# One value piece split by DMA engines, and the bias in five transfers: attention decode with a dense layer on one core

## The chip, the cores and the metric

The kernel runs on one core of a Trainium2 chip. The metric is device time in microseconds (us) of one execution. Before the change three runs took 191.95, 192.65 and 192.1 us; the median is 192.1 us.

## What is computed

One token for each of two sequences goes through a layer norm. Its result feeds an attention over the last 4096 positions of a key and value cache, and a dense layer with the mish activation. Both results are added to the input.

```python
def reference(A_x, A_k_cache, A_v_cache, A_wq, A_wo, B_x, B_w1, B_b1, B_w2):
    def _A_ref(x, k_cache, v_cache, wq, wo):
        ...
        W = min(4096, max(256, Sk // 4))
        q = (x @ wq).reshape(B, Sq, Hq, Dh).transpose(0, 2, 1, 3)
        k = jnp.repeat(k_cache[:, :, Sk - W:, :], rep, axis=1)
        v = jnp.repeat(v_cache[:, :, Sk - W:, :], rep, axis=1)
        p = _softmax(jnp.einsum("bhqd,bhkd->bhqk", q, k) * (Dh ** -0.5), axis=-1)
        o = jnp.einsum("bhqk,bhkd->bhqd", p, v)
        return o.transpose(0, 2, 1, 3).reshape(B, Sq, Hq * Dh) @ wo
    def _B_ref(x, w1, b1, w2):
        h = jnp.einsum("bsd,df->bsf", x, w1) + b1
        ...
        return jnp.einsum("bsf,fd->bsd", h * jnp.tanh(sp), w2)
    xn = _layernorm(A_x, axis=-1)
    return A_x + _A_ref(xn, ...) + _B_ref(xn, ...)
```

The sizes: two sequences, width 448, 16 query heads on 8 key heads of 256 values, 4096 positions, and 1792 hidden values in the dense layer; all in bf16.

## The kernel before

The work on the cache is cut into four units (`U`, two key heads of both sequences each, so `J` = 4 rows of the cache). In a unit the keys come in four pieces (`load_k`, L91) and the values in four (`load_v`, L97), each a tile of 128 partitions by 16 KB, 2 MB in all. A value piece `g` holds 1024 positions: partition `4x + j` has 32 tokens in a row (`T`) of the block `x` (32 blocks, `C`) of cache row `j`. All pieces go through rings of buffers: three for keys, four for values, two for wo. `wq` and `w1` borrow buffers of the value ring and `w2` one of the key ring.

The order is written out by hand (`manual_schedule`, L65), and nearly all transfers stand in one queue, that of SP, in the order of the code: two key pieces, wq in two parts, a key piece, w1, a key piece; then for every unit (the loop at L569) the four value pieces, the keys of the next unit, and its part of wo (`load_wo`, L106). In the last unit wo goes first, in two transfers, value piece 3 comes in two parts (L577, L578), and w2 in four parts ends the stream (L580, `load_w2` at L537). Only x and the bias b1 are issued from ACT (L122, L124). The framework gives every transfer one of eight semaphores in turn, so a transfer is issued when the eighth before it has landed. Where it writes a used buffer, it also waits for the buffer's reader.

The compute engines follow the stream. DVE turns every key piece (`turn`, L264, the transposes of L267); PE makes the scores (`scores`, L342), ACT their exponential (L351), DVE turns them (L357). PE then weighs the values: `values` (L381, matmul L389) piece by piece, in matmuls of two tokens each, and `gather` (L400) folds the result. In the last unit, piece 3 takes another way (`values_fixed`, L419, matmul L424), `finish` (L433) divides by the softmax's sum, `mix` (L479) multiplies by wo and `dense_out` (L548) adds the dense layer's second half part by part; both record their matmuls at L247. DVE and ACT copy the result out (L620, L622) and SP stores it (L623).

At the start ACT loads x and the bias and computes the root for the layer norm (L158); DVE goes on from there with small steps to `xs` (L161 to L218), which PE needs for the projection (L289) and for the dense layer's first half (L501). The bias is used at L515, by DVE, after the four key pieces of unit 0 have been turned.

Of the kernel before, what the change touches and what calls it, by code (L numbers as in the profile page):

```python
# [17 lines left out]
def kernel(  # L18
# [13 lines left out]
    nc = tc.nc  # L32
    P = 128
    G = 4
    J = 4
# [3 lines left out]
    _, Hkv, Sk, Dh = A_k_cache.shape  # L39
# [8 lines left out]
    C = P // J  # L48
    CT = W // C
    T = CT // R  # L50
# [35 lines left out]
    def ring(name):  # L86
        return v_pool.tile([P, KE], BF16, tag="v", name=name)
# [3 lines left out]
    def load_k(u, r):  # L91
        t = k_pool.tile([P, KE], BF16, tag="k", name="k")
        src = kview[u][:, s0:, :].rearrange("j (c t) d -> c j (t d)", c=C)
        nc.sync.dma_start(out=t[:], in_=src[:, :, r * KE : (r + 1) * KE])  # L94
        k_t[u, r] = t

    def load_v(u, g, lo=0, hi=T):  # L97
        if lo == 0:
            v_t[u, g] = ring("v")
        t = v_t[u, g]  # L100
        src = vview[u][:, s0:, :].rearrange("j (g x t) d -> g x j (t d)", g=G, x=C)
        nc.sync.dma_start(
            out=t[:, lo * Dh : hi * Dh], in_=src[g, :, :, lo * Dh : hi * Dh]
        )

    def load_wo(u):  # L106
        w = wo_pool.tile([P, KU, rep, 2 * D], BF16, tag="wo", name="wo")
        if u < U - 1:
            nc.sync.dma_start(
                out=w[:].rearrange("p k h e -> p (k h e)"),  # L110
                in_=A_wo.rearrange("(k u y i) d -> u y k (i d)", k=KU, u=U, i=8)[u],
            )
        for k2 in range(KU if u == U - 1 else 0):
            r0 = (u + U * k2) * rep * Dh
            nc.sync.dma_start(  # L115
                out=w[:, k2, :, :],
                in_=A_wo[r0 : r0 + rep * Dh, :].rearrange("(h p c) d -> p h (c d)", h=rep, p=P),
            )
        wo_t[u] = w
# [1 line left out]
    x_bf = consts.tile([Bsz, D], BF16)  # L121
    nc.scalar.dma_start(out=x_bf[:, :], in_=A_x.flatten_outer_dims())  # L122
    b1_sb = consts.tile([P, 2, NI], BF16)
    nc.scalar.dma_start(out=b1_sb[:], in_=B_b1.rearrange("(k q c) -> q k c", k=2, q=P))  # L124

    load_k(0, 0)
    load_k(0, 1)
# [2 lines left out]
    for lo, hi in ((0, 4), (4, NS)):  # L130
        t = ring("wq")
# [14 lines left out]
    for k in range(KU):  # L146
        nc.gpsimd.tensor_copy(
            out=hot[:, k, :, :, k], in_=ident[:].rearrange("p (q y) -> p y q", y=4)
# [10 lines left out]
        out=rstd[:], in_=mv[:, 1:2], func=ACT.Sqrt, bias=eps_t[:], scale=1.0  # L159
# [4 lines left out]
        out=xn_bf[:],  # L164
# [8 lines left out]
        out=parm[:], in_=ident[:].rearrange("p (a o) -> p o a", o=2), axis=AXIS.X, op=ALU.add  # L173
# [3 lines left out]
        out=jm[:],  # L177
        in_=ident[:].rearrange("p (a j h) -> p j a h", j=J, h=rep),
# [4 lines left out]
        out=jm[:], in0=jm[:], scalar1=-1.0, scalar2=29952.0, op0=ALU.add, op1=ALU.mult  # L183
# [3 lines left out]
        out=mneg[:], in_=jm[:].unsqueeze(1).to_broadcast([P, TH * 8, J])  # L187
    )
    sel = consts.tile([P, 2, NQ], FP32)
    for x in range(2):  # L190
        for w in range(4):
            at = 32 * w + (2 * (w % 2) + x) * NQ
            src = ident[:, at : at + NQ]
            if w == 0:
                nc.vector.tensor_copy(out=sel[:, x, :], in_=src)
            else:
                nc.vector.tensor_tensor(
                    out=sel[:, x, :], in0=sel[:, x, :], in1=src, op=ALU.add
# [16 lines left out]
    for odd in range(2):  # L215
        for half in range(2):
            o = (half + odd) % 2
            nc.vector.tensor_scalar(  # L218
                out=xs[:, odd::2, half * Bsz : (half + 1) * Bsz],
# [12 lines left out]
    def carry():  # L232
        e_sb = small.tile([P, 2 * Dh], FP32, tag="vs", name="e_sb", bufs=1)[0:Bsz, 0:D]
        nc.scalar.copy(out=e_sb, in_=early[:])
        for g in range(G):
            nc.tensor.matmul(
                acc[32 * g : 32 * g + Bsz, :],
                lhsT=id2[:],
                rhs=e_sb[:, g * DG : (g + 1) * DG],
                start=True,  # L240
                stop=False,
                skip_group_check=True,
            )
# [31 lines left out]
    for n in range(2):  # L275
        for e in range(2):
# [3 lines left out]
                out=sp[:],  # L280
                in_=ident[:, o : o + 63 : 2].unsqueeze(1).to_broadcast([P, G, 32]),
# [47 lines left out]
    def scores(u, i):  # L329
        sc = ps_sc.tile([P, TH, 32], FP32, tag="sc", name="sc")  # L330
        nc.tensor.matmul(  # L331
            sc[:].rearrange("p t m -> p (t m)"),
            lhsT=ident[:],
            rhs=mneg[:].rearrange("p a j -> p (a j)"),
            start=True,
            stop=False,
            skip_group_check=True,
        )
        for n in range(NB):
            for e in range(2):  # L340
                for w in range(4):
                    nc.tensor.matmul(  # L342
                        sc[32 * w : 32 * (w + 1), :, :],
                        lhsT=qd[:, u, 2 * n + e, :, :].rearrange("p g q -> p (g q)"),
                        rhs=ktm[i][:, n, e, :, 32 * w : 32 * (w + 1)],
                        start=False,
                        stop=(n == NB - 1 and e == 1),
                        skip_group_check=True,
                    )
        ex = small.tile([P, TH, 32], BF16, tag="ex", name="ex")  # L350
        nc.scalar.activation(  # L351
            out=ex[:].rearrange("p t m -> p (t m)"),
            in_=sc[:].rearrange("p t m -> p (t m)"),
            func=ACT.Exp,
            scale=scale,
        )
        nc.vector.transpose(  # L357
            out=p_t[i][:].rearrange("p g t q -> p t g q"),
            in_=ex[:].rearrange("p t (g q) -> p t g q", g=G),
        )  # L360
# [84 lines left out]
    def relay(u):  # L445
        oT = state.pop(("oT", u))
        ox_ps = ps_m.tile([P, 4, 2, Bsz], FP32, tag="m", name="ox_ps")
        for h in range(rep):
            rows = slice(h * 64, (h + 1) * 64)
            for y in range(4):  # L450
                for k in range(KU):
                    nc.tensor.matmul(  # L452
                        ox_ps[rows, y, :, :],
                        lhsT=hot[:, k, y, :, :].rearrange("p q k -> p (q k)"),
                        rhs=oT[:, :, k * rep + h, :],
                        start=(y == 0 and k == 0),
                        stop=(y == 3 and k == KU - 1),
                        skip_group_check=True,
                    )
        ox = small.tile([P, 8, Bsz], BF16, tag="ox", name="ox")  # L460
        nc.scalar.copy(
            out=ox[:].rearrange("p i b -> p (i b)"),
            in_=ox_ps[:].rearrange("p y c b -> p (y c b)"),
        )
        state["ox", u] = ox

    def mix_early(u):
        ox = state.pop(("ox", u))
        w = wo_t.pop(u)[:].rearrange("p k h (c d) -> p (k h c) d", c=2)
        for i in range(8):  # L470
            nc.tensor.matmul(  # L471
                early[:],
                lhsT=ox[:, i, :],
                rhs=w[:, i, :],
                start=False,
                stop=(u == U - 2 and i == 7),
            )
# [59 lines left out]
    def load_w2(part):  # L537
        if part == 0:
            state["w2"] = k_pool.tile([P, KE], BF16, tag="k", name="w2")
        k, lo, hi = w2_parts[part]  # L540
        w2_in = B_w2.flatten().rearrange("(k p e) -> k p e", k=2, p=P)
        at = k * NI * D
        nc.sync.dma_start(
            out=state["w2"][:, at + lo * D : at + hi * D],
            in_=w2_in[k, :, lo * D : hi * D],
        )
# [9 lines left out]
    def turns(u, r):  # L556
        for i in range(NH):
            turn(u, r, i)
# [10 lines left out]
    for u in range(U):  # L569
        last = u == U - 1  # L570
        if last:
            load_wo(u)
        load_v(u, 0)
        load_v(u, 1)
        load_v(u, 2)
        if last:
            load_v(u, 3, 0, 24)  # L577
            load_v(u, 3, 24, T)  # L578
            for part in range(len(w2_parts)):
                load_w2(part)  # L580
        else:
            load_v(u, 3)
            load_k(u + 1, 0)
            load_k(u + 1, 1)
            load_k(u + 1, 2)
            load_wo(u)
            load_k(u + 1, 3)
        if u > 0:
            relay(u - 1)
            mix_early(u - 1)  # L590
        if last:
            carry()
        scores(u, 0)
        scores(u, 1)
        weigh(u)
        for g in range(G - 1):
            values(u, g)
        if not last:
            values(u, G - 1)
            turns(u + 1, 0)  # L600
            turns(u + 1, 1)
            gather(u)
            finish(u)
            turns(u + 1, 2)
            turns(u + 1, 3)
    u = U - 1
# [9 lines left out]
    for g in range(G):  # L616
        dst = res[:, g * DG : (g + 1) * DG]
        src = acc[32 * g : 32 * g + Bsz, :]
# [35 lines left out]
```

The softmax here doesn't subtract the row's maximum and nothing guards it: scores larger than these inputs give would overflow.

## Time and profile before

| What | Value |
|---|---|
| Median of three runs | 192.1 us |
| The profiled execution's own time | 192.14 us |
| Its span (first to last instruction) | 190.1 us |
| PE busy | 79.8 us (42%) |
| DVE busy | 91.5 us (48%) |
| ACT busy | 12.3 us (6%) |
| DMA | 77.79 MB, mean 409 GB/s |
| Issue of a value piece on SP (L102), last unit | 541 ns median, five issues from 150.6 to 156.2 us |
| Issue of a part of w2 on SP (L543) | 337 ns median, four issues from 161.2 to 168.4 us |
| Issue of the bias on ACT (L124) | 404 ns; 12.7 us to landing |

Times in the views are microseconds from the span's start. A view by windows gives the busy time of every engine in a stretch, then the clock that was granted to TensorE, the mean busy share of the 16 DMA engines and what they moved. DMA packets are listed by queue: q1 has the transfers that SP issues, q10 those of ACT, q8 and q14 carry instructions. The trace has times and sizes of the packets, but not the number of the engine that moved one. For a transfer it has the times at which its engines report: sixteen events on its semaphore, here called landings.

### The profile page before, as it was taken

How to read it: one execution, taken by the hardware profiler on the slowest of the kernel's cores; microseconds unless marked ns; L12 is line 12 of the kernel's file. 1: busy time of each engine (PE TensorE's matmuls, PEld its weight loads, DVE VectorE, ACT ScalarE, POOL GpSimd, SP SyncE). 2: the span in 40 equal slices, each digit the busy share in tenths (PEclk: the TensorE clock that was granted, in tenths of full speed). 3: DMA queues.
4: the chain of work that ended last, by engine and by line, in shares of the span. 5: the costliest groups of instructions: out<-in, count | busy, mean ns of one | idle time of the engine just before them, and what ended most of it. 6: DMA issues, size and time to landing. Idle time of an engine off the chain costs nothing.

```text
span 190.1 us, 2021 instructions
## 1 busy us (share of the span) xinstructions
PE 79.8 (42%) x873; PEld 37.8 (20%) x873; DVE 91.5 (48%) x97; ACT 12.3 (6%) x23; POOL 4.0 (2%) x16
## 2 busy tenths in 40 slices
PE   0301525197316016296233017394252026575384
PEld 0100115032104012032014012131022021221182
DVE  6887067583001999553003996823006994831001
ACT  3000030011001000011001000020010001020001
POOL 8000000000000000000000000000000000000000
PEclk9999999999965555869955555889755557696555
DMA  6999999999999999999999999999999999999990
GB/s 221 390 435 427 442 418 434 424 422 428 428 431 428 421 427 425 431 434 424 424 428 428 434 421 428 428 431 421 438 424 421 422 433 400 434 428 418 416 377 29
DMA packets 7025, 77.79 MB, mean 409 GB/s; under 512 B 997, under 2 KB 1769, under 8 KB 2537
## 3 DMA queue, kind: packets, MB, share of 16 engines
q1 hardware_dynamic: 6740, 77.66, 96.8%
q8 instruction: 6, 0.10, 0.2%
q10 hardware_dynamic: 276, 0.01, 0.1%
q14 instruction: 3, 0.02, 0.0%
HBM read 77.67 MB, written 0.00 MB: 409 GB/s over the span
## 4 chain that ended last, share of the span: by engine, by line
DMA 85%; DVE 10%; issue 3%; SPq 1%; PE 0%; DVEq 0%
DMA k<-in_A_k_cache_dram 66%; DMA w<-in_B_w_dram 12%; DVE kt L267 10%; DMA wo<-in_A_wo_dram 7%; PE acc L247 0%; SPq L115 0%; SPq L94 0%; DVEq L649 0%; DVE res L620 0%; DVE oT L436 0%
## 5 line engine op out<-in xcount | busy, mean ns | idle before, releaser
L267 DVE STREAM_TRANSPOSE kt<-k 128x2048 f32<-128x2048 f32 x32 | 72.1, 2290 | 55.5 <-DMA k<-in_A_k_cache_dram 55.4
L389 PE MATMUL pv<-v,p 128*32 128x512 bf16 x240 | 19.4, 462 | 25.7 <-DMA v<-in_A_v_cache_dram 25.7
L342 PE MATMUL sc<-kt,qd 128*32 128x512 bf16 x256 | 22.0, 500 | 13.9 <-DVE kt L267 13.9
L389 PEld LDWEIGHTS <-p 128*32 128x32 bf16 x240 | 7.0, 107 | 41.3 <-issue 37.8
L452 PE MATMUL ox_ps<-oT,hot 128*64 128x4 bf16 x48 | 2.3, 192 | 29.7 <-DVE oT L436 29.7
L342 PEld LDWEIGHTS <-qd 128*32 128x32 bf16 x256 | 8.5, 115 | 25.5 <-issue 23.1
L357 DVE STREAM_TRANSPOSE p<-ex 128x512 bf16<-128x512 bf16 x8 | 5.7, 712 | 13.1 <-ACT ex L351 13.1
L471 PE MATMUL early<-wo,ox 128*2 128x448 bf16 x24 | 9.4, 571 | 5.1 <-DMA wo<-in_A_wo_dram 5.1
L409 PE MATMUL o<-sel,vs 128*128 128x8 f32 x32 | 7.5, 363 | 2.9 <-ACT vs L403 2.9
L409 PEld LDWEIGHTS o<-sel,vs 128*128 128x128 f32 x32 | 7.1, 325 | 6.5 <-ACT vs L403 6.5
L289 PE MATMUL q_ps<-wq,xs 128*32 128x512 bf16 x28 | 3.4, 624 | 12.0 <-DMA wq<-in_A_wq_dram 12.0
L452 PEld LDWEIGHTS <-hot 128*64 128x64 bf16 x48 | 2.5, 151 | 29.6 <-issue 29.5
L351 ACT ACTIVATE ex<-sc 128x512 bf16<-128x512 f32 x8 | 4.8, 597 | 39.6 <-PE sc L342 39.6
L436 DVE TENSOR_TENSOR oT<-o,rec 128x16 bf16<-128x16 f32 x4 | 0.6, 145 | 12.7 <-PE o L424 12.7
L403 ACT COPY vs<-pv 128x512 f32<-128x512 f32 x4 | 2.3, 586 | 49.8 <-PE pv L389 49.8
L367 PE MATMUL dn<-p,ones 128*128 128x512 bf16 x8 | 3.1, 383 | 4.5 <-DVE p L357 4.5
L501 PE MATMUL h_ps<-xs,w 128*128 128x4 bf16 x49 | 2.8, 193 | 4.9 <-DMA w<-in_B_w_dram 4.9
L471 PEld LDWEIGHTS <-ox 128*2 128x2 bf16 x24 | 2.8, 115 | 9.6 <-issue 8.5
L331 PE MATMUL sc<-mneg,ident 128*128 128x512 bf16 x8 | 4.1, 514 | 0.0
L210 PE MATMUL xr_ps<-ident,xrows 2*128 2x2 bf16 x7 | 1.0, 180 | 6.6 <-DVE xrows L209 6.6
L289 PEld LDWEIGHTS <-xs 128*32 128x32 bf16 x28 | 1.0, 126 | 13.9 <-issue 13.9
L306 DVE COPY qT<-qt_ps 128x16 bf16<-128x16 bf16 x4 | 0.4, 167 | 6.9 <-PE qt_ps L301 6.9
(62 smaller groups left out, 39.9 us busy)
## 6 DMA issues: line engine op xcount, KB each, us to landing
k<-in_A_k_cache_dram SPq DMA_DIRECT2D x16, 2048.0 KB, 18.0
v<-in_A_v_cache_dram SPq DMA_DIRECT2D x15, 2048.0 KB, 25.1
wo<-in_A_wo_dram SPq DMA_DIRECT2D x3, 896.0 KB, 31.4
wq<-in_A_wq_dram SPq DMA_DIRECT2D x1, 2048.0 KB, 16.2
w<-in_B_w_dram SPq DMA_DIRECT2D x1, 1568.0 KB
wq<-in_A_wq_dram SPq DMA_DIRECT2D x1, 1536.0 KB, 19.3
v<-in_A_v_cache_dram SPq DMA_DIRECT2D x1, 1536.0 KB, 27.8
wo<-in_A_wo_dram SPq DMA_DIRECT2D x2, 448.0 KB, 13.2
```

The lines of the kernel that those rows point to most:

```text
L267: nc.vector.transpose(out=kt[i][:, :, :, r, :], in_=t[:, i * w : (i + 1) * w].bitcast(FP32).rearrange("p (a c j) -> p a c j", c=P // (R * ...
L289: nc.tensor.matmul(q_ps[32 * u : 32 * (u + 1), :], lhsT=xs[:, s, :], rhs=wq_t[s][:, u * 512 : (u + 1) * 512], start=(s == 0), stop=(s == N ...
L331: nc.tensor.matmul(sc[:].rearrange("p t m -> p (t m)"), lhsT=ident[:], rhs=mneg[:].rearrange("p a j -> p (a j)"), start=True, stop=False, ...
L342: nc.tensor.matmul(sc[32 * w : 32 * (w + 1), :, :], lhsT=qd[:, u, 2 * n + e, :, :].rearrange("p g q -> p (g q)"), rhs=ktm[i][:, n, e, :, 3 ...
L351: nc.scalar.activation(out=ex[:].rearrange("p t m -> p (t m)"), in_=sc[:].rearrange("p t m -> p (t m)"), func=ACT.Exp, scale=scale,)
L357: nc.vector.transpose(out=p_t[i][:].rearrange("p g t q -> p t g q"), in_=ex[:].rearrange("p t (g q) -> p t g q", g=G),)
L367: nc.tensor.matmul(dn[:].rearrange("p a q -> p (a q)"), lhsT=ones[:], rhs=p_t[i][:].rearrange("p g t q -> p (g t q)"), start=(i == 0), sto ...
L389: nc.tensor.matmul(pv[32 * w : 32 * (w + 1), :, :].rearrange("p x d -> p (x d)"), lhsT=p_t[a // 4][:, g, 4 * (a % 4) : 4 * (a % 4) + 4, :] ...
L409: nc.tensor.matmul(po[:, c, :], lhsT=sb[:, x, c::2], rhs=sel[:, x, :], start=(x == 0 and c == 0), stop=(last and x == 1), skip_group_check ...
L452: nc.tensor.matmul(ox_ps[rows, y, :, :], lhsT=hot[:, k, y, :, :].rearrange("p q k -> p (q k)"), rhs=oT[:, :, k * rep + h, :], start=(y == ...
L471: nc.tensor.matmul(early[:], lhsT=ox[:, i, :], rhs=w[:, i, :], start=False, stop=(u == U - 2 and i == 7),)
L501: nc.tensor.matmul(h_ps[:, i, :, :].rearrange("p k b -> p (k b)"), lhsT=w1_v[:, s, i, :], rhs=xs[:, s, 0 : 2 * Bsz], start=(s == 0), stop= ...
```

## The change

Value piece 0 of the last unit was one transfer of 32 tokens on 128 partitions. Now its first 26 tokens are one such transfer, and the other six come in four transfers of 32 partitions each (8 blocks by 4 cache rows, 3 KB on a partition). [...] The bias, one transfer of 128 partitions before, comes in five: one of 64 partitions and four of 16. Nothing else is changed; the bytes moved are the same.

```diff
-    def load_v(u, g, lo=0, hi=T):
-        if lo == 0:
+    def load_v(u, g, lo=0, hi=T, x0=0, x1=C):
+        if lo == 0 and x0 == 0:
             v_t[u, g] = ring("v")
         t = v_t[u, g]
         src = vview[u][:, s0:, :].rearrange("j (g x t) d -> g x j (t d)", g=G, x=C)
         nc.sync.dma_start(
-            out=t[:, lo * Dh : hi * Dh], in_=src[g, :, :, lo * Dh : hi * Dh]
+            out=t[J * x0 : J * x1, lo * Dh : hi * Dh], in_=src[g, x0:x1, :, lo * Dh : hi * Dh]
         )
...
-    nc.scalar.dma_start(out=b1_sb[:], in_=B_b1.rearrange("(k q c) -> q k c", k=2, q=P))
+    b1_in = B_b1.rearrange("(k q c) -> q k c", k=2, q=P)
+    for lo, hi in ((0, 64), (64, 80), (80, 96), (96, 112), (112, P)):
+        nc.scalar.dma_start(out=b1_sb[lo:hi], in_=b1_in[lo:hi])
...
-        load_v(u, 0)
+        if last:
+            load_v(u, 0, 0, 26)
+            for x0 in range(0, C, 8):
+                load_v(u, 0, 26, T, x0, x0 + 8)
+        else:
+            load_v(u, 0)
         load_v(u, 1)
         load_v(u, 2)
```

## The prediction

> **What bounds the kernel now.** I read the page's slices and queues first, then the chain that ended last, then the windows of the last microseconds, the instructions there, and last the queue of SP.
>
> The slices, the queues and the chain of the page:
>
> ```profile
> DMA  6999999999999999999999999999999999999990
> q1 hardware_dynamic: 6740, 77.66, 96.8%
> q8 instruction: 6, 0.10, 0.2%
> q10 hardware_dynamic: 276, 0.01, 0.1%
> DMA 85%; DVE 10%; issue 3%; SPq 1%; PE 0%; DVEq 0%
> ```
>
> The DMA engines are busy from the second slice to the last but one, and the chain is 85% DMA. The kernel is one stream of 77.66 MB on q1, and all else hides behind it. So a part of the change counts only if it alters the moment at which the stream ends, or adds work behind that moment. Two rows matter beside q1: q8 moves six packets of instructions, 0.10 MB or 16 KB each, and q10 is the small queue of x and the bias.
>
> How the stream ends, in windows (PE, PEld, DVE, ACT, POOL busy, clock, DMA share, GB/s):
>
> ```profile
> 184.00:184.50 0.50, 0.43 (x17) 0.34 (x13) 0.03 (x1) 0.00 (x0) 0.00 (x0) 0.50 1.14 425
> 184.50:185.00 0.50, 0.30 (x16) 0.30 (x20) 0.14 (x1) 0.00 (x0) 0.00 (x0) 0.50 0.70 264
> 185.00:185.30 0.30, 0.30 (x24) 0.30 (x16) 0.00 (x0) 0.00 (x0) 0.00 (x0) 0.50 0.39 155
> 185.30:185.60 0.30, 0.30 (x28) 0.30 (x20) 0.00 (x0) 0.00 (x0) 0.00 (x0) 0.50 0.34 131
> 185.60:186.00 0.40, 0.40 (x32) 0.40 (x21) 0.00 (x0) 0.00 (x0) 0.00 (x0) 0.50 0.35 130
> 186.60:187.00 0.40, 0.35 (x8) 0.01 (x3) 0.00 (x0) 0.00 (x0) 0.00 (x0) 0.50 0.00 0
> ```
>
> The share falls from full to about 0.35 by 185.3 and stays there until 186: six of sixteen engines still have data. The semaphore events of the trace say the same of each transfer. The last one's sixteen landings are ten from 185.00 to 185.34, then 186.22, 186.48, 186.64, 186.66, 186.86 and 186.95. The lag is old: landings show two late engines at 41 us, three at 66, four at 97, five at 133, six from 168 on. Each step follows a packet on an instruction queue (q14 at 39.7 with 8 KB; q8 at 36.0, 60.3, 91.6, 128.2, 163.6 with 16 KB, about 1.1 us each). A sixth q8 packet, at 184.5, delays none of the landings.
>
> What runs behind the stream (start, time, what):
>
> ```profile
> 178.22 1.90 PE L389 MATMUL pv<-v,p 128*32 128x512 bf16 x16 [2.99 <-DMA v<-in_A_v_cache_dram]
> ...
> 182.58 1.85 PE L424 MATMUL o<-p,v 128*128 128x8 bf16 x64
> 184.47 0.17 DVE L436 TENSOR_TENSOR oT<-o,rec 128x16 bf16<-128x16 f32 x1 [12.74 <-PE o L424]
> ...
> 184.70 0.91 PE L247 MATMUL acc<-wo,oT 128*2 128x112 bf16 x32 [0.27 <-DVE oT L436]
> ```
>
> PE waits for value piece 2 (landed at 178.18) and then works almost without a gap to 187.45. Its last 56 matmuls need about 1.6 us at the 28 ns of the 32 before them, from 185.6 on, so without the last DMA waits it would end near 187.2. Two things thus end together: the stream and PE's work from piece 2 on. Both follow the slow engines, since piece 2 has the same gap (ten landings by 176.56, six up to 178.18).
>
> [...] x, with two rows, has two data packets and two landings. [...] the bias packets lie one between every two 16 KB packets from 4.3 to 13 us. [...]
>
> **The change, part by part.** The sum is made against the profiled execution: 192.14 us, span 190.1, 2.0 around it; the median of the runs shown is 192.1, the same within 0.1.
>
> Value piece 0 of the last unit. Prices are packet start to packet start on one engine: 607 ns for 16384 bytes, 456 for 12288, so 494 for 13312 (26 tokens, between the two); 3072 bytes lie between 1792 (70) and 3584 (136), so 117; the closing 4-byte packet 6.
> - Before, every engine: 8 x 607 = 4.86 us.
> - After, engines 8 to 15: 8 x 494 = 3.95, which is 0.91 less.
> - After, engines 0 to 7: 3.95 + 4 transfers x 4 packets x 117 + 4 x 6 = 5.85, which is 0.99 more.
> Nothing comes between this piece and the end that evens the engines out, so the shift passes whole to piece 2 and to the last transfer.
>
> SP issues four more transfers of 0.54 us (the row of value issues). Every transfer also waits for the eighth before it, by its semaphore. So piece 1 waits for the last key piece (161.1), piece 2 and the first part of 3 for the two wo transfers (162.3, 163.5), the second part and the four w2 transfers for piece 0 and its four small ones (near 168). Before, w2 went out from 161.2 to 168.4; now to about 170. Engines take up piece 1 near 166 and w2 near 183, so over 4 and about 13 us cover it; past that, it would be paid one for one. The output's wait is long over.
>
> Bias. ACT issues four more of 0.40 us: table load and rstd (L158, ending at 3.4) come 1.6 us later, and DVE behind them: its row of small steps ends near 10.0 instead of 8.36, and the first transposes (8.43 to 17.92) shift by as much. Behind these wait PE's projection (idle until wq lands at 18.3) and the issue of key piece 3 (at 12.96, needed at 30.6). DVE waits for the third key piece at 26.87 anyway. Cost nil, cover about 8 us. The bias itself has 16 data packets per engine as before and 4 more closing ones, landing near 17 instead of 14, needed at 40. By the ring of eight, wq part 2 waits for key piece 0 (8.4), key piece 2, w1 and key piece 3 for bias pieces (10 to 15 us): all with over 4 MB queued ahead, and none needed before 18. 8 new transfers in all leave the end's order on the semaphores as it was, but for the small pieces. PE's program and so its q8 packets stay.
>
> So the whole effect is one question: on which side are the six late engines? No row of the profile numbers an engine. Had chance put them, all six among 8 to 15 would be very rare (28 in 8008)[...]. And one of the six was hit by q14[...]. The bounds of the unknown:
> - all six in 8 to 15: late ones end at 186.95 - 0.91 = 186.04, the others at 185.34 + 0.99 = 186.33. 0.62 earlier.
> - the least late one (186.22) in 0 to 7: 187.21, 0.26 later. The middle ones (186.48 to 186.66): 187.5 to 187.65, up to 0.70 later.
> - the latest in 0 to 7: 187.94, 0.99 later.
> [...]
>
> I take both sides, with a middle engine or the least late one in 0 to 7: 0.26 to 0.70, middle 0.5. 192.14 + 0.5 = 192.6.
>
> **The rivals.**
> - Gain: all late engines are the relieved ones. For it: six fit into eight[...]. Against: two queues, and six of eight places. 192.14 - 0.62 = 191.5.
> - Slower, clearly: the latest engine is among 0 to 7, which already end the stream and now carry 0.99 more. It decides from the point where an engine of 0 to 7 lands after 186.9 before the change; price 0.99[...]: 193.1 to 193.8. For it: nothing says that instructions prefer the upper half. Against: only one or two of the sixteen are that late.
> - It doesn't do what it says: the pieces spread over all sixteen engines. Then each has the old bytes and eight more closing or short packets, under 0.1: 192.2. Against it: x's two packets.
>
> **How the numbers follow.** Forecast 0.44 (192.4 to 192.9); gain 0.30 (191.3 to 191.8); slower 0.20 (193.1 to 193.8); nothing 0.06. A measurement of this kernel tells about 0.5%, 0.96 us, from no change: below 191.1 or above 193.1. The gain reaches that only with luck in the runs (they spread over 0.7): 0.04. Slower: 0.20 of the rival and 0.02 of the forecast's tail. Same: 0.74. The range holds gain and forecast and the lower half of the slower case: 191.4 to 193.4. The forecast's own range is 192.4 to 192.9.
>
> **What would show it.** In the last windows, the DMA share would again end in a long step if late engines were loaded, or fall within 0.4 us if they were relieved. The landings of piece 2 and of the last transfer tell the groups: 0.99 later for eight, 0.91 earlier for eight. SP's w2 issues should end near 170, rstd near 5, with key landings up to 158 as before. I am wrong if PE's matmuls at L389 wait less at piece 2 though the stream ends no earlier, if early landings move by over 0.3, or if the small transfers take much more than 117 ns a packet.

## The result, and the profile after

The changed kernel takes 194.64 us (median of six runs, 193.68 to 194.83) where the kernel before takes 192.26 (191.95 to 192.65): a ratio of 1.011, with a 95% interval from 1.009 to 1.014. It is 2.4 us slower. The profiled execution took 194.63 us with a span of 192.9, which is 2.8 more than before. What lies around the span is 1.7 instead of 2.0.

The page of the changed kernel, slices, queues and chain:

```profile
DMA  5999999999999999999999999999999999999960
q1 hardware_dynamic: 6900, 77.66, 96.0%
q8 instruction: 6, 0.10, 0.2%
q10 hardware_dynamic: 340, 0.01, 0.1%
DMA 76%; DVE 11%; PE 5%; issue 3%; ACTq 2%; ACT 1%; SPq 0%; DVEq 0%
```

The bytes of q1 are the same; there are 160 packets more, and 64 closing packets more on q10. Each of the four small transfers has eight landings, so it ran on eight engines. The prediction and the expectations call these engines 0 to 7 and the others 8 to 15; no trace numbers them, and the numbers are names here. That it is the same eight each time is seen with the extra transfers below: four of them to partitions 0 to 63 make eight landings of the next piece 1.7 us later and the other eight 0.2. The chain has gained PE (5%) and lost DMA. The stream is still the bound up to its end, but more stands behind that end.

The same stretch in windows (PE, PEld, DVE, ACT, POOL busy, clock, DMA share, GB/s):

```profile
185.50:186.00 0.50, 0.50 (x25) 0.50 (x22) 0.00 (x0) 0.00 (x0) 0.00 (x0) 0.50 0.78 305
186.00:186.50 0.50, 0.23 (x15) 0.15 (x15) 0.17 (x1) 0.00 (x0) 0.00 (x0) 0.50 0.84 312
186.50:187.00 0.50, 0.50 (x28) 0.50 (x32) 0.00 (x0) 0.00 (x0) 0.00 (x0) 0.50 0.40 133
187.00:187.40 0.40, 0.40 (x28) 0.40 (x20) 0.00 (x0) 0.00 (x0) 0.00 (x0) 0.50 0.09 34
187.40:187.70 0.30, 0.30 (x24) 0.30 (x16) 0.00 (x0) 0.00 (x0) 0.00 (x0) 0.50 0.06 24
187.70:188.20 0.50, 0.50 (x32) 0.41 (x21) 0.00 (x0) 0.00 (x0) 0.00 (x0) 0.50 0.06 23
188.20:188.70 0.50, 0.26 (x12) 0.08 (x1) 0.00 (x0) 0.00 (x0) 0.00 (x0) 0.50 0.01 2
188.70:189.20 0.50, 0.00 (x0) 0.00 (x0) 0.00 (x0) 0.00 (x0) 0.00 (x0) 0.50 0.00 0
```

Before, the share stood near 0.35 (six engines) until 186 and then ran out by 186.6. Now nearly all engines are busy until 186.5, and from 187.4 to past 188 the share is 0.06: one engine of sixteen. The landings of the last transfer say it too: three at 185.29 to 185.64, eleven from 186.85 to 187.32, one at 187.64, one at 188.68.

In the last window PE does nothing either, though all data is there. The instructions of that time, and the last lines of the chain:

```profile
187.14 1.32 PE L249 MATMUL acc<-w,act_bf 128*2 128x112 bf16 x44
189.23 0.45 PE L249 MATMUL acc<-w,act_bf 128*2 128x112 bf16 x12 [0.77 <-DMA w<-in_B_w_dram]
189.23 0.18 PEld L249 LDWEIGHTS <-act_bf 128*2 128x2 bf16 x11 [0.95 <-issue]
189.70 0.56 DVE L627 CAST res<-acc 2x112 bf16<-2x112 f32 x2 [3.32 <-PE acc L249]
189.74 0.51 ACT L629 CAST res<-acc 2x112 bf16<-2x112 f32 x2 [7.19 <-PE acc L249]
190.75 0.29 SPq L630 DMA_DIRECT2D out_dram<-res  x1
```
```profile
186.44 2.02 PE acc L249 x47
188.46 0.77 issue
189.23 0.49 PE acc L249 x12
```

The timeline puts the matmuls' gap down to the DMA of w2. But eight of these twelve matmuls work on w2's third part, which landed at 188.44, and four on its last, which landed at 188.68, 0.55 us before they start. The weight load in front of them waited for nothing that the profile shows ("issue"), and so says the chain. The copies end at 190.27, and SP issues the output only at 190.75. So two stalls follow the stream. From these times, for both profiled executions:

| Step | Before | After | Difference |
|---|---|---|---|
| last landing of w2 | 186.95 | 188.68 | +1.73 |
| then to the start of the last matmuls | 0.04 | 0.55 | +0.51 |
| then to the end of the copies | 1.00 | 1.04 | +0.04 |
| then to the issue of the output | 0.06 | 0.48 | +0.42 |
| then to the output's landing | 1.17 | 1.26 | +0.09 |
| then to the end of the span | 0.87 | 0.84 | -0.03 |

The sum is +2.76, the whole difference of the spans. The experiments take the rows with 1.73, 0.51 and 0.42 one after the other.

### The profile page after: what moved, and what is told of

The parts are those of the page before. It is cut to its first block, busy times and chain, and to the rows that moved or that the text cites. A ratio compares the mean times of both kernels' runs of the same rounds, so it can differ in the third digit from the quotient of the medians.

```text
span 192.9 us, 2031 instructions
## 1 busy us (share of the span) xinstructions
PE 81.5 (42%) x872; PEld 37.9 (20%) x873; DVE 91.3 (47%) x97; ACT 12.3 (6%) x23; POOL 3.9 (2%) x16
## 4 chain that ended last, share of the span: by engine, by line
DMA 76%; DVE 11%; PE 5%; issue 3%; ACTq 2%; ACT 1%; SPq 0%; DVEq 0%
DMA k<-in_A_k_cache_dram 60%; DVE kt L269 9%; DMA v<-in_A_v_cache_dram 9%; DMA wo<-in_A_wo_dram 7%; ACTq L126 1%; PE acc L249 1%; PE pv L391 1%; PE o L411 1%; PE o L426 1%; ACT L160 1%; DVE sel L199 1%; PE xr_ps L212 1%; DVE xs L220 0%; ACT vs L405 0%; ACTq L122 0%
## 5 line engine op out<-in xcount | busy, mean ns | idle before, releaser
L391 PE MATMUL pv<-v,p 128*32 128x512 bf16 x240 | 20.4, 479 | 25.4 <-DMA v<-in_A_v_cache_dram 25.4
L344 PE MATMUL sc<-kt,qd 128*32 128x512 bf16 x256 | 22.7, 511 | 13.9 <-DVE kt L269 13.9
L503 PEld LDWEIGHTS <-w 128*128 128x128 bf16 x49 | 2.7, 154 | 5.0 <-DMA w<-in_B_w_dram 5.0
L377 DVE TENSOR_REDUCE rec<-dn 128x8 f32<-128x512 f32 x4 | 2.8, 692 | 1.9 <-PE dn L369 1.9
```

The source lines that it names most:

```text
L344: nc.tensor.matmul(sc[32 * w : 32 * (w + 1), :, :], lhsT=qd[:, u, 2 * n + e, :, :].rearrange("p g q -> p (g q)"), rhs=ktm[i][:, n, e, :, 3 ...
L391: nc.tensor.matmul(pv[32 * w : 32 * (w + 1), :, :].rearrange("p x d -> p (x d)"), lhsT=p_t[a // 4][:, g, 4 * (a % 4) : 4 * (a % 4) + 4, :] ...
L503: nc.tensor.matmul(h_ps[:, i, :, :].rearrange("p k b -> p (k b)"), lhsT=w1_v[:, s, i, :], rhs=xs[:, s, 0 : 2 * Bsz], start=(s == 0), stop= ...
```

## The experiments

Each kernel is compared with the kernel before as it ran beside it (192.25 to 192.34 us). Times are medians, and a ratio is the time over that of the kernel before.

Four theories are tested first. P: the uneven shares of the engines, made worse since the pieces for partitions 64 to 127 and the transfers of the other eight engines slow each other; this was an assumption, which no run had shown yet. Q: the later start of ACT and DVE, or the shifted order of the semaphores. R: small packets or more transfers are dearer than priced. S: the source blocks 16 to 31 are slow to read. E, I and F came later and are told where they are tested.

### The parts alone

Bias in five, the value piece whole:

> The kernel before with only the bias in five transfers. Theory P (engines 0 to 7 carry more, one of them was already late[...]): nothing at the end, 192.3 us, within 0.3. Theory Q (the loss comes from the longer start of ACT and DVE, or from the shifted ring of semaphores): at least 193.

The pieces alone, the bias whole:

> The changed kernel with the bias in one transfer again. Theory P: the whole loss, 194.5 us, and the first transposes at 8.4 us as before. Theory Q: about 192.6.

The same bytes in as many transfers, but over all engines:

```diff
-            for x0 in range(0, C, 8):
-                load_v(u, 0, 26, T, x0, x0 + 8)
+            for lo, hi in ((26, 28), (28, 30), (30, 31), (31, T)):
+                load_v(u, 0, lo, hi)
```

> The changed kernel, but the six tokens come in four transfers of 128 partitions on all sixteen engines (2, 2, 1 and 1 tokens). Theory P: no loss, 192.3 us. Theory R (small packets, or four more transfers as such, are dearer than priced): over 193.5.

| Kernel | Time, us | Ratio, 95% interval | Last landing of w2 | Span |
|---|---|---|---|---|
| bias in five alone | 192.86 | 1.0017 to 1.0039 | 186.63 | 190.7 |
| pieces alone | 194.94 | 1.0121 to 1.0161 | 189.29 | 193.1 |
| over all engines | 192.94 | 1.0023 to 1.0046 | 186.99 | 191.1 |

The pieces alone carry the whole loss, as P expected. The stream is late only where they go to eight engines: placement, not number or size of transfers. But the first and the last lose 0.6 to 0.7 us with a stream that ends when it did (186.95 before). P expected nothing there and Q at least 0.7 for the bias; the loss stands behind the last landing, which neither theory had in it. R falls with the third run: as many transfers, with packets of 512 and 1024 bytes where the change has 3072, and no later end of the stream.

### Which engines, and what slows them

The changed kernel with the pieces in another order, partitions 64 to 127 first (`for x0 in (16, 24, 0, 8)`):

> The changed kernel with the four pieces in another order: those for partitions 64 to 127 first, those for 0 to 63 last. Theory P: the same time as the changed kernel, 194.6 within 0.4, but the long steps between the landings (1.0 and 0.85 us, the last two pieces before) now belong to the first two pieces, and the last two step by 0.5. Theory R: the steps keep their order, the last two long.

It takes 194.85 us (ratio 1.0097 to 1.0156), as P expected. In the changed kernel the on-time engines land the four pieces near 166.1, 166.7, 167.7 and 168.5: steps of 0.6, 1.0 and 0.8 us. In this one they land near 166.8, 167.6, 168.1 and 168.7: the piece at place two, here one for partitions 64 to 127, takes 0.9, and the two for 0 to 63 take 0.5 and 0.6. The long steps moved with the pieces.

To part destination from source, four extra transfers of the same form (32 partitions x 3 KB, 8 engines) go into an unread buffer behind a whole value piece in the kernel before, once to partitions 0 to 63 from the blocks that the changed kernel loads to 64 to 127, once the other way round:

```diff
         load_v(u, 0)
+        if last:
+            load_spare(u, ((0, 16), (32, 24), (0, 16), (32, 24)))
```

The pairs are first partition and first source block; each transfer takes tokens 26 to 31 of its eight blocks. The other kernel has ((64, 0), (96, 8), (64, 0), (96, 8)).

> The kernel before plus four extra transfers that nobody reads, behind value piece 0 of the last unit, of the changed kernel's shape (32 partitions, 3 KB each, engines 0 to 7), into a spare buffer: all to partitions 0 to 63, read from the source blocks 16 to 31. Theory P[...]: steps of 0.5 us between their landings, eight landings of piece 1 about 1.9 us later, the other eight unmoved; the latest of engines 0 to 7 ends the stream, about 193.5 us. Theory S (the source blocks 16 to 31 make a piece slow): steps of 0.85 to 1.0.

> The same with the places turned round: all four extra transfers go to partitions 64 to 127 and read the source blocks 0 to 15. Theory P: steps of 0.85 to 1.0 us, all sixteen landings of piece 1 later, about 195.5 us, clearly over the one with low partitions. Theory S: steps of 0.5 and the same time as the one with low partitions.

| Extra transfers to | Time, us | Ratio, 95% interval | One transfer | Their eight engines, next piece | The other eight, next piece |
|---|---|---|---|---|---|
| partitions 0 to 63 | 193.72 | 1.0056 to 1.0086 | 0.46 to 0.49 | +1.7 | +0.2 |
| partitions 64 to 127 | 196.72 | 1.0215 to 1.0265 | 0.87 to 0.96 | +3.9 | +2.1 |

The last two columns are the on-time landings of value piece 1 against those of before (171.30 to 171.66). The windows of the two kernels in the time of these transfers, low first:

```profile
166.50:168.00 1.50, 1.50 (x17) 0.33 (x13) 0.02 (x1) 0.60 (x1) 0.00 (x0) 0.67 1.06 434
168.00:170.00 2.00, 1.96 (x33) 0.77 (x22) 0.69 (x1) 0.30 (x1) 0.00 (x0) 1.00 0.98 416
```
```profile
166.50:168.00 1.50, 1.50 (x13) 0.24 (x9) 0.11 (x1) 0.60 (x1) 0.00 (x0) 0.50 1.00 210
168.00:170.00 2.00, 2.00 (x28) 0.80 (x24) 0.60 (x1) 0.00 (x0) 0.00 (x0) 0.62 1.10 247
```

In both the sixteen engines are busy all the time (share 1.0), but with the high destination they move about half: 210 and 247 GB/s instead of 434 and 416. A busy share tells that packets are under way, not how fast. A transfer to the high partitions takes 0.87 to 0.96 us, one to the low 0.46 to 0.49. The other eight engines, which have no part in it, lose 2.1 us with the high destination, about 0.5 for each of the four, and 0.2 in all with the low one.

No trace says which partitions an engine writes, and none shows why the destination counts. What is measured is that transfers to partitions 64 to 127 take twice the time beside whole pieces, and that both groups of engines lose by it (3.9 and 2.1 us, against 1.7 and 0.2). P is confirmed in this; of its two times, 193.5 and 195.5, the first was met and the second passed by 1.2 us. S falls: blocks 16 to 31 are quick when they go to low partitions, and blocks 0 to 15 slow when they go to high ones.

The changed kernel shows the same in the time of its own pieces. The first line is of the kernel before, the others of the changed one:

```profile
168.00:170.00 2.00, 1.25 (x21) 0.42 (x10) 0.47 (x2) 0.60 (x1) 0.00 (x0) 1.00 1.02 434
166.00:167.00 1.00, 1.00 (x13) 0.16 (x5) 0.00 (x0) 0.00 (x0) 0.00 (x0) 0.50 1.05 263
167.00:168.00 1.00, 1.00 (x15) 0.34 (x17) 0.32 (x1) 0.60 (x1) 0.00 (x0) 0.77 1.26 301
168.00:169.00 1.00, 1.00 (x24) 0.44 (x20) 0.40 (x1) 0.00 (x0) 0.00 (x0) 1.00 0.71 261
```

### What is lost behind the last landing

Of SP's instructions in the trace, one comes some 0.45 us late although what it waits for is there: the 80th of those recorded. In the kernel before, the 80th is the wait for the output, the last of five waits at the end, and the output is under way until 189.22 anyway. The five instructions that the pieces add (four issues and a wait) bring the output's own issue onto this place (theory I). To test it, ACT issues the output:

```diff
-    nc.sync.dma_start(out=out.flatten_outer_dims(), in_=res[:])
+    nc.scalar.dma_start(out=out.flatten_outer_dims(), in_=res[:])
```

In the changed kernel, and as a control in the kernel before:

> The changed kernel with its output issued by ACT instead of SP. In the changed kernel SP issues the output 0.49 us after its data is ready, in the kernel before 0.06 us. Theory I (a place in SP's own instruction stream stalls it for about 0.45 us; five more instructions ahead of it have brought the output's issue onto that place): the output goes out within about 0.1 us of the last copy, time about 194.2 (-0.4). If the issue is late because of the data or of the queue of semaphores, it stays at 194.6 with the gap of 0.5.

> The kernel before with its output issued by ACT instead of SP, the control of the changed kernel's run with the same edit. Theory I expects no gain, since SP there has its stall behind the output's issue, while the output is under way: about 192.3 (within 0.2). A gain of 0.4 here as well would mean that ACT's issue is simply quicker than SP's.

The changed kernel takes 194.19 us (ratio 1.0074 to 1.0111), 0.45 less than with SP. That interval overlaps the one with SP (1.0088 to 1.0137), so the medians alone don't show the gain. The trace shows that the wait is gone: the output goes out 0.08 us after the copies, which end at 190.33:

```profile
189.80 0.51 ACT L629 CAST res<-acc 2x112 bf16<-2x112 f32 x2 [7.17 <-PE acc L249]
190.41 0.28 ACTq L630 DMA_DIRECT2D out_dram<-res  x1
```

The control was expected at 192.3 and takes 192.92 (1.0017 to 1.0045). With the output's issue gone SP has fewer instructions ahead of the 80th, which now comes behind the output's landing (189.39): the gap is from 189.49 to 189.92 there, and the span ends 1.33 us after the landing instead of 0.87. The expectation was wrong, since I had forgotten that the edit moves the place; the place itself was confirmed. (The other 0.2 is the matmuls' stall told below: 0.29 here, 0.04 in the kernel before.) Where it falls in each trace:

| Kernel | Gap ahead of SP's instruction | What it holds up |
|---|---|---|
| before | 80 of 85 | the wait for the output: hidden |
| after; over all engines | 80 of 90 | the output's issue: 0.45 |
| after, output by ACT | 80 of 88 | a wait for w2: hidden |
| before, output by ACT | 80 of 83 | the end: 0.43 |
| bias in five alone | 80 of 85 | the end: 0.43 |
| the four extra transfers, either way | 80 of 91 | a wait for a value piece: hidden |

The bias in five leaves SP's program as it was, and yet it shows the gap. There the reason is the order of the end (theory E, a form of Q). SP waits at the end for the transfer semaphores in a fixed order, with five instructions. Four more transfers move the output to another semaphore, which is waited for first; the other four waits, 0.07 us each, and the gap come behind its landing (189.17) instead of ahead of it: the span ends 1.55 us after the landing. To test this, four transfers of 2 rows x 64 bytes behind the whole bias; and the bias in five with those four ahead of it, eight more in all:

```diff
+    for n in range(4):
+        x_more = consts.tile([Bsz, 32], BF16, name=f"x_more{n}")
+        nc.scalar.dma_start(out=x_more[:, :], in_=A_x.flatten_outer_dims()[:, 0:32])
```

> The kernel before, bias whole, with four transfers of 2 rows x 64 bytes into unused tiles issued by ACT behind the bias. The run with the bias in five cost about 0.6 us with a stream that ended no later. Theory E (order of the end): four more transfers move the output's completion to another of the eight semaphores on which SP waits at the very end, and SP waits for it first, with four more waits of about 0.07 us and a gap of about 0.45 us behind it instead of ahead of it. It expects about 192.9 (+0.6) here too, the output landing at about 189.2 as before and the span ending 1.5 us after that instead of 0.9. Theory B (splitting the bias itself costs, by its packets or by rstd being late): about 192.3, 0.9 us between landing and end.

> The kernel before with the bias in five transfers, and the four transfers of 2 rows x 64 bytes ahead of them: eight more in all, so that the output's completion falls on its old place among the eight semaphores. Theory E expects about 192.3 (no change), the span ending 0.9 us after the output's landing. Theory B expects the 192.9 of the bias in five, or more, since ACT starts later still (rstd near 8).

The first takes 192.96 us (1.0017 to 1.005), as much as the bias in five, though its bias is whole. The four transfers make ACT later too (its table load starts at 3.40 instead of 1.74), but the stream ends no later for it (186.80), and the span ends 1.55 us after the output's landing at 189.35: the loss stands at the end. The second ends 0.86 after it, as expected, but takes 193.18 (1.0032 to 1.0058). Its stream is late by 0.6 (last landing at 187.55): with ten transfers on ACT, SP's second key piece is issued at 6.67 instead of 1.44, behind the semaphore of the eighth transfer before it. So the order is confirmed by the end of the trace, not by the time.

In the changed kernel both parts add up to eight, and the output is waited for last. With the pieces alone it is waited for first, and the span ends 1.11 us after its landing instead of 0.84; this is a part of why the pieces alone (194.94) are no quicker than the whole change.

### The last matmuls

Theory F is that the last matmuls wait for the last packet of instructions. 20 small matmuls at 10 us, where PE waits for wq, shift its program against the 16 KB packets on q8:

```diff
     early = ps_e.tile([Bsz, D], FP32)
+    for _ in range(20):
+        nc.tensor.matmul(
+            early[:, 0:32], lhsT=ident[0:Bsz, 0:Bsz], rhs=x_bf[:, 0:32],
+            start=True, stop=False, skip_group_check=True,
+        )
```

> The changed kernel with 20 small extra matmuls (2 x 32 columns, overwritten afterwards) on PE at about 10 us, where PE waits for wq. They shift PE's blocks of instructions by 20 matmuls. In the changed kernel the last 12 matmuls start at 189.23, 0.55 us after their data landed (188.68) and 2.55 us after the start of the last 16 KB instruction packet (186.68); in the kernel before 2.49 us after it. Theory F (these matmuls wait for that packet): with the packet some 20 matmuls (about 1.2 us) earlier, the last group starts within 0.1 us of the last landing; about 194.1 (-0.5), or no gain [...] in which case the start still follows the packet by 2.4 to 2.6 us. If PE is late for another reason, the gap of 0.5 stays whatever the packet does.

The last one has this and the output by ACT:

> The changed kernel with both edits, the output issued by ACT and the 20 extra matmuls early on PE. Theories I and F together: 0.4 and 0.5 less, about 193.7, which leaves the stream's own 1.7 over the kernel before (192.3 + 1.7 = 194.0, less what the kernel before loses itself at its end). If the whole loss were the stream's, 194.6 stays.

| Kernel | Last landing of w2 | Last packet on q8 starts | Last matmuls start | After the landing | After the packet |
|---|---|---|---|---|---|
| before | 186.95 | 184.50 | 186.99 | 0.04 | 2.49 |
| bias in five alone | 186.63 | 184.53 | 186.95 | 0.32 | 2.42 |
| over all engines | 186.99 | 185.14 | 187.56 | 0.57 | 2.42 |
| four tiny transfers | 186.80 | 184.78 | 187.13 | 0.33 | 2.35 |
| eight more transfers | 187.55 | 185.57 | 188.02 | 0.47 | 2.45 |
| before, output by ACT | 186.89 | 184.73 | 187.18 | 0.29 | 2.45 |
| after | 188.68 | 186.68 | 189.23 | 0.55 | 2.55 |
| after, output by ACT | 188.87 | 186.74 | 189.29 | 0.42 | 2.55 |
| extra transfers, low | 188.48 | 184.76 | 188.52 | 0.04 | 3.76 |
| after, 20 matmuls | 188.74 | 183.60 | 188.78 | 0.04 | 5.18 |
| after, both edits | 188.88 | 183.63 | 188.92 | 0.04 | 5.29 |

The last matmuls are those behind the last gap. Where their start follows the packet, these are the eight on w2's third part (in some kernels all but the first of them) and the four on its last; in the last three rows only the four, as the eight have run before. In the last two rows the packet is the one at 183.6; another, at 188.01, is too late to matter.

The three kernels left out fit too. With the pieces alone the eight start 2.55 us after the packet, 0.24 after the landing of their own part, and the four follow them. With the extra transfers to high partitions all but the first of the eight start 2.40 after the packet, and the four 0.04 after their landing; with the high pieces first, both groups start 0.04 after theirs. So in these traces a group starts at the latest of three moments: 0.04 us after the landing of its own part, 2.35 to 2.55 after the packet, or behind the group before it.

The kernel before has this stall too. There all but the first of the eight stand until 186.99, though their part landed at 186.70; as the last part lands at 186.95, most of the stall is hidden. PE ends 0.49 us after the last landing there, 0.99 after it in the changed kernel, and 0.30 or 0.31 after it in the last three rows. The end of the chain of the run over all engines shows the stall where the stream is not late (the last landing is at 186.99):

```profile
186.74 0.04 issue
186.78 0.25 PE acc L249
187.03 0.53 issue
187.56 0.45 PE acc L249 x10
```

In the changed kernel with the 20 matmuls the packet comes 3 us earlier, where 1.2 was expected, and the stall is gone:

```profile
188.51 0.36 PEld L254 LDWEIGHTS <-act_bf 128*2 128x2 bf16 x11 [0.21 <-issue]
189.07 0.56 DVE L632 CAST res<-acc 2x112 bf16<-2x112 f32 x2 [2.64 <-PE acc L254]
```

The copies start at 189.07 instead of 189.70, and the profiled execution's span is 192.2 instead of 192.9. But the median does not follow: 194.75 (ratio 1.0115 to 1.0146). The profiled run was the quickest of four (194.11; the others 194.74 to 194.87). With both edits it is 194.28 (1.0077 to 1.0112), with the profiled run again the quickest of five (193.64). So the traces show that the stall goes when the packet comes earlier. That it costs the median 0.5 us is not shown: most runs with the packet moved are as slow as those without, and there is no trace of them. In the two traces the last landing hardly moves (188.74 and 188.88 against 188.68).

Why the packet starts when it does stays open. The earlier ones start when 778, 641, 515, 384 and 271 records of weight loads (waits among them) are still ahead (kernel before), some 127 apart; by that step the last would be due with 144 ahead, at 182.9 before and 184.6 after. It starts 1.6 and 2.1 us later, and no run shows the cause.

No version beat the kernel before.

## Why the prediction was wrong

The forecast was 192.6, within 191.4 to 193.4; the result is 194.64. The span grew by 2.76 us where 0.5 was forecast: the stream ends 1.73 later, and 0.93 stands behind its end, for which nothing was kept. By its steps:

- **The bound.** Right: one stream, six late engines, and only what moves its end or stands behind it counts. The windows ended in a long step, as was said for the case that late engines are loaded.
- **Prices of the pieces.** Nearly right for partitions 0 to 63: 0.5 to 0.6 us in the changed kernel and 0.46 to 0.49 with the extra transfers there, where 4 packets x 117 ns = 0.47 were priced. The first landings of the 26 tokens come 0.90 earlier than those of the 32 before (165.51 instead of 166.41), where 0.91 was priced.
- **The placing.** Seven of the eight engines of the small transfers are on time in the landings of the first piece (166.00 to 166.18) and one is late (167.64): the late engines lie on both sides, the case I took. By its landing of the 26 tokens (166.71; the least late of before, 167.60, less 0.91 is 166.69) it is most likely the least late one, for which "187.21, 0.26 later" was forecast. It ended at 188.68.
- **The failed step: the destination.** The sum prices all four pieces alike, at 4 packets x 117 ns, whatever partitions they go to. The two pieces to partitions 64 to 127 take 1.0 and 0.8 us instead of 0.47 each. The on-time engines of the eight come about 1.9 us later to piece 1 (173.20 to 173.49 instead of 171.30 to 171.66), where 0.99 was priced. The other eight lose more than they were spared: the late ones land the 26 tokens at 168.05 to 168.36, about where they landed 32 before, and the three that are on time land piece 1 some 0.3 later than before (171.62 to 171.96). Any forecast of a gain was gone with this.
- **The late engine's own price.** The late one of the eight took 0.93, 0.84, 1.06 and 0.85 us for the four pieces (the first of these rests on its likely landing above), 3.68 in all where the sum has 1.9. The two high pieces took 1.0 more than priced, about what they cost the on-time engines too (0.9), and the two low ones 0.8 more. That these were slow too, while the other engines were at the high ones, no run explains; with the extra transfers to low partitions a late engine took 0.48 for each. So it came to piece 1 at 170.39, 2.79 us later than the least late engine before, and it ended the stream 2.46 later (188.68 against 186.22), where 0.99 was forecast. The number of late ones isn't fixed either: with the high pieces first, two are among the eight (168.32 and 169.51 in the first piece, the others by 166.96), and the last landing is at 189.60.
- **"PE's program and so its q8 packets stay."** Right as to the program, wrong as to its weight. I read that the sixth packet "delays none of the landings" and left it there. But the last matmuls start no earlier than 2.35 us after it where they follow it. Before, the last data landed (186.95) just before that moment (186.99, 2.49 after the packet); now the packet decides: 0.5 us in the profiled run. And of PE's last waits before, which the prediction took for DMA waits, the 0.24 us up to 186.99 are the packet's.
- **SP's four issues at nothing.** The cover was there, and w2's issues ended at 170.97, near the 170 forecast. What was missed is that instructions also move those behind them: 0.45 us at the output's issue, gone from the trace when ACT issues it.
- **Bias at nothing.** Right in its early part: rstd came late (5.56 us where near 5 was forecast), DVE's small steps ended at 10.78, and the last key landings (159.13 to 161.02) stayed. ACT took 2.92 us for five issues, where 0.40 each was priced. Alone it costs 0.6, all behind the last landing and the most of it by the output's place among the semaphores. That eight more transfers leave that order as it was, as the prediction said, is what keeps this out of the changed kernel.
- **The range.** The rival "slower, clearly" was 193.1 to 193.8, at most 1.7 over the 192.14 of the sum. The stream alone came to 1.73. Nothing was kept for the 0.9 behind it, since only the stream's end and PE's work were taken to set the end.

## What to carry to other kernels

Before giving engines uneven shares of a transfer, measure what the destination partitions cost: eight engines that sent to partitions 64 to 127 beside whole pieces took 0.87 to 0.96 us for a transfer instead of 0.46 to 0.49, and the other eight lost 2.1 us with them. Read the end of a stream to the last instruction: here a stall in PE's instructions took up to 0.57 us of a trace there, one in SP's 0.45, and waits placed behind the output's, with that stall, about 0.7 (the span ended 1.55 us after the output's landing instead of 0.87). A few more instructions or transfers moved them. Where a busy share stays full, read the GB/s beside it.

## What the runs showed of the hardware

- While eight engines sent the four extra transfers to partitions 64 to 127 beside whole pieces, the sixteen moved 210 to 247 GB/s with a busy share of 1.0 to 1.1; while they sent them to partitions 0 to 63, 416 to 434 with a share of 0.98 to 1.06.
- Where the last groups of matmuls followed the last 16 KB packet on q8, they started 2.35 to 2.55 us after its start, though the packet itself took 0.97 us (before and after the change); up to 0.57 us of this stood open behind the last landing.
- SP had one place, ahead of the 80th recorded instruction, where it stood for 0.43 to 0.45 us in every trace where no wait hid it.
- The waits of SP at the end cost about 0.07 us each here, and came in the order of the semaphores, whichever transfer was last.
